# Blocks of 512 columns for the second stretch of a weight conversion, and two lasting buffers for the 16-bit exponentials in place of three

## Chip, cores and metric

One NeuronCore of one Trainium2 chip. The metric is the device time of one execution in microseconds, over all engines, from the first instruction to the last. Lower is better.

## What is computed

Three operations in a row, all in float32 at the borders, with batch 2, 768 positions, 8 heads of 64:

```python
mask = q_bucket[:, :, :, None] == k_bucket[:, :, None, :]
scores = np.where(mask, scale * q @ k.T, -1e9)
x = softmax(scores) @ v                      # (2, 768, 512) after joining heads
u = x + real(fft(fft(x, axis=1), axis=2))
un = (u - mean(u)) / sqrt(var(u) + 1e-6)
u = u + relu(un @ w_ch1) @ w_ch2             # 512 -> 2048 -> 512
out = (sigmoid(conv(u, conv_w)) * (u @ w_val)) @ w_out
```

The buckets are the signs of six projections of q and of k. The matrix products run on pairs of 16-bit numbers (a high part and the rest, three products for one), so that the result keeps the accuracy of float32. The weights arrive as 64-bit floats, read as pairs of 32-bit words.

## The kernel before

The program is written once per batch half b = 0, 1. For each half the attention runs over four head pairs g, each with three blocks i of 256 positions and two heads hh. `pair` (L312) does one head of one block: scores on TensorE (L320), their maximum on VectorE (L330), the exponential on ScalarE (L333) into `e`, then a 16-bit copy on ScalarE (L112, `a<-e`) and the rest `e - a` on GpSimd (L120, `a<-e,a`) in two halves, for each of two rows j. The finished tile `a` is transposed by a DMA from SP's queue (L346, `at<-a`). `unit_out` (L349) multiplies two transposed tiles with the values (L355, 36 matmuls), which ends a block; there are 12 blocks in each half. `prep` (L230) makes the 16-bit q and k of the next head pair in a tile `st` from the same pool as `a`, also transposed by a DMA (L247, `tb<-st`), and the bucket rows (L259, L264).

The tiles come from pools in two parts. The base part is there for both halves of the batch; `widen` adds buffers that exist for the first attention alone, and `Pool.tile` takes base and added buffers in turn. Before the change `a` has three base buffers and one added one, `at` two and two, `e` two and one.

After the attention of half 0 the mixing (`back`, L515), the norm (`norm`, L618), and the feed-forward (`ffn`, L679: first product L703, eviction L684 and L685, second product L720, eviction L691) of half 0 run beside the attention of half 1. Later come the mixing of half 1, the gating of half 0, and the feed-forward and gating of half 1.

The weights are converted in two stretches by `weights` (L414). One block is loaded into a ring by SP (L424), and for each part of a block three integer steps on VectorE (`widen`, L410 to L412) make a float32 tile `wt` from the two words. Then `split` brings it to scale and makes the two 16-bit parts:

```python
t = pool.tile([128, wp], INT32, tag="wt", name="wt", bufs=2)
k = (name, i * (r.shape[1] // wp) + c // wp)
with after_mark([marks[GATES[k]]] if k in GATES else last if PACE and not name else []):
    marks[k] = widen(t, r[:, cl, 0], r[:, cl, 1], t).ins
split(h[:, cl], l[:, cl], t.bitcast(FP32), s, how[k[1] % len(how)])
```

The first stretch takes most of `w_ch1` beside the first attention, in 12 blocks of 512 columns. The second stretch (named `w2`) takes the remaining 512 columns of `w_ch1` and all of `w_ch2` beside the mixing of half 0 and the attention of half 1, in 40 blocks of WP = 256 columns with a ring of two slots. Its `split` is "aag": two ScalarE steps (L112, `wt<-wt` and `w<-wt`) and one on GpSimd (L120, `w<-wt,w`).

What sets the order: a planner reorders each engine's instructions by dependencies and its own estimate of times. `after_mark` gives it extra edges that only bind the order; `GATES` names such edges for single blocks of the conversion (a block may not stand before a mark such as the end of the first attention, `(0, "unit", 2)`, or the first norm, `(0, "norm", 0)`). Each engine and SP's queue then work strictly in the order they are given.

## Time and profile before

| | |
|---|---|
| runs shown | 707.6, 707.6 and 710.81 us, median 707.6 |
| the profiled execution's own time | 703.61 us |
| its span | 701.8 us |
| TensorE busy | 572.9 us (82%) |
| VectorE busy | 534.5 us (76%) |
| ScalarE busy | 350.9 us (50%) |
| GpSimd busy | 313.2 us (45%) |
| mean granted TensorE clock | 0.903 |

The span is the time from the first to the last instruction in the trace; 1.8 us lie around it. Busy times are sums over the whole span, which has stages with different limits, so they say little by themselves. Windows over the span give each stage its own shares; the chain of waits follows the last instruction back to what released it.

### The profile page before, as it was taken

How to read it: one execution, taken by the hardware profiler on the slowest of the kernel's cores; microseconds unless marked ns; L12 is line 12 of the kernel's file. 1: busy time of each engine (PE TensorE's matmuls, PEld its weight loads, DVE VectorE, ACT ScalarE, POOL GpSimd, SP SyncE). 2: the span in 40 equal slices, each digit the busy share in tenths (PEclk: the TensorE clock that was granted, in tenths of full speed). 3: DMA queues.
4: the chain of work that ended last, by engine and by line, in shares of the span. 5: the costliest groups of instructions: out<-in, count | busy, mean ns of one | idle time of the engine just before them, and what ended most of it. 6: DMA issues, size and time to landing. Idle time of an engine off the chain costs nothing.

```text
span 701.8 us, 12761 instructions
## 1 busy us (share of the span) xinstructions
PE 572.9 (82%) x4958; PEld 436.3 (62%) x4958; DVE 534.5 (76%) x1002; ACT 350.9 (50%) x731; POOL 313.2 (45%) x321
## 2 busy tenths in 40 slices
PE   5775576666664769988789999799989999999997
PEld 2334353444343547666567789678767788888864
DVE  5799797997999998999875629996799346182582
ACT  4576767883866445776578725321434302121142
POOL 5665959795577722876556431455232100000000
PEclk8557878868975799999989999999999999999999
DMA  3989999999578552676875884200000000000001
GB/s 118 203 233 222 238 236 223 215 221 204 139 151 179 135 144 65 146 165 148 163 133 109 157 159 151 91 1 2 0 31 31 32 1 1 1 2 1 1 31 61
DMA packets 191804, 79.72 MB, mean 114 GB/s; under 512 B 176384, under 2 KB 182144, under 8 KB 191744
## 3 DMA queue, kind: packets, MB, share of 16 engines
q1 hardware_dynamic: 191168, 78.81, 50.6%
q8 instruction: 39, 0.64, 0.4%
q10 hardware_dynamic: 576, 0.10, 0.1%
q14 instruction: 21, 0.17, 0.1%
HBM read 32.50 MB, written 3.15 MB: 51 GB/s over the span
## 4 chain that ended last, share of the span: by engine, by line
PE 33%; DVE 27%; DMA 6%; issue 5%; POOL 4%; ACT 2%; SPq 1%; ACTq 0%; DVEq 0%; POOLq 0%
PE f L720 12%; PE f L703 10%; DMA at<-a 3%; DVE wt L412 3%; PE pv L355 2%; DVE sc L330 2%; DVE wt L411 2%; DVE wt L410 2%; DVE gt L745 2%; PE op L864 2%; POOL a L120 2%; DVE z L120 2%; DMA ring<-in_moe_w_ch_dram 2%; DVE h L685 1%; PE vp L839 1%
## 5 line engine op out<-in xcount | busy, mean ns | idle before, releaser
L120 POOL TENSOR_TENSOR a<-e,a 128x384 f16<-128x384 f32 x184 | 183.5, 1021 | 90.6 <-ACT a L112 50.6
L703 PE MATMUL f<-un,w 128*128 128x256 f16 x1152 | 134.6, 274 | 5.0 <-DVE h L685 4.7
L720 PE MATMUL f<-h,w 128*128 128x256 f16 x1152 | 132.3, 273 | 0.9 <-POOL w L120 0.9
L703 PEld LDWEIGHTS <-w 128*128 128x128 f16 x1152 | 112.7, 98 | 24.0 <-issue 7.2
L720 PEld LDWEIGHTS <-w 128*128 128x128 f16 x1152 | 111.5, 98 | 16.2 <-POOL w L120 1.4
L355 PE MATMUL pv<-at,vt 128*64 128x256 f16 x864 | 77.7, 335 | 31.3 <-DMA at<-a 21.0
L330 DVE TENSOR_SCALAR_CACHE_REDUCE sc<-sc 128x768 f32<-128x768 f32 x96 | 91.4, 961 | 14.4 <-PE sc L320 13.2
L355 PEld LDWEIGHTS <-vt 128*64 128x64 f16 x864 | 62.0, 136 | 56.4 <-issue 38.7
L333 ACT ACTIVATE e<-sc,mx 128x768 f32<-128x768 f32 x96 | 85.5, 891 | 4.1 <-POOL a L120 1.2
L320 PE MATMUL sc<-ta 96*128 96x384 f16 x192 | 54.4, 367 | 39.0 <-ACT e L333 28.6
L112 ACT ACTIVATE a<-e 128x768 f16<-128x768 f32 x96 | 79.9, 839 | 11.1 <-DMA at<-a 7.9
L685 DVE SCALAR_TENSOR_TENSOR h<-f,h 128x512 f16<-128x512 f32 x48 | 32.6, 684 | 34.4 <-ACT h L684 34.2
L320 PE MATMUL sc<-tb 128*128 128x384 f16 x192 | 56.1, 376 | 0.0
L684 ACT ACTIVATE h<-f 128x512 f16<-128x512 f32 x48 | 28.4, 591 | 49.2 <-PE f L703 49.0
L320 PEld LDWEIGHTS <-ta 96*128 96x128 f16 x192 | 17.5, 103 | 56.3 <-issue 42.0
L120 POOL TENSOR_TENSOR w<-wt,w 128x256 f16<-128x256 f32 x40 | 36.1, 910 | 32.6 <-ACT w L112 32.4
L112 ACT ACTIVATE x<-xb 128x256 f16<-128x256 f32 x24 | 11.8, 534 | 67.3 <-DVE xb L691 66.9
L331 ACT ACTIVATE mx<-mx 128x1 f32<-128x1 f32 x96 | 18.8, 197 | 52.7 <-DVE sc L330 48.1
L412 DVE SCALAR_TENSOR_TENSOR wt<-ring,wt 128x256 int32<-128x256 int32 (+1 forms) x60 | 43.3, 728 | 0.4
L691 DVE SCALAR_TENSOR_TENSOR xb<-f,xb 128x256 f32<-128x256 f32 x24 | 13.7, 615 | 37.6 <-PE f L720 37.6
L411 DVE SCALAR_TENSOR_TENSOR wt<-ring,wt 128x256 int32<-128x256 int32 (+1 forms) x60 | 41.3, 696 | 0.5
L812 DVE SCALAR_TENSOR_TENSOR gt<-xb,cw,gt 128x256 f32<-128x256 f32 x60 | 37.1, 673 | 0.0
(144 smaller groups left out, 905.5 us busy)
## 6 DMA issues: line engine op xcount, KB each, us to landing
ring<-in_moe_w_ch_dram SPq DMA_DIRECT2D x40, 256.0 KB, 3.0
ring<-in_moe_w_ch_dram SPq DMA_DIRECT2D x12, 512.0 KB, 4.4
lv<-in_v_dram SPq DMA_DIRECT2D x8, 384.0 KB, 3.7
out_dram<-ob SPq DMA_DIRECT2D x12, 256.0 KB, 2.0
lq<-in_q_dram SPq DMA_DIRECT2D x7, 384.0 KB, 3.8
lk<-in_k_dram SPq DMA_DIRECT2D x7, 384.0 KB, 4.2
ring<-in_moe_w_val_dram SPq DMA_DIRECT2D x4, 512.0 KB, 4.2
ring<-in_moe_w_out_dram SPq DMA_DIRECT2D x4, 512.0 KB, 3.5
```

What stands on the lines that cost most here:

```text
L112: return nc.scalar.activation(out=o, in_=i, func=ACTF.Copy, scale=s)
L120: return (nc.gpsimd if eng == "g" else nc.vector).tensor_tensor(out=o, in0=i0, in1=i1, op=op)
L320: nc.tensor.matmul(out=s[:, n, 0:384], lhsT=z[0:rows, 0, hh, r], rhs=z[0:rows, 1, hh, n * 384:n * 384 + 384], start=(x == 0), stop=(x == 1),)
L330: last[:] = [nc.vector.tensor_scalar(s, s, -(PEN * PEN) / 2, None, ALU.max, ALU.max, accum_out=m[:, 0:1]).ins]
L333: marks["first", 2 + j] = nc.scalar.activation(out=e.rearrange("p (a b) -> p a b", a=2), in_=s, func=ACTF.Exp, bias=m[:, 1:2], scale=SC, a ...
L355: nc.tensor.matmul(out=p[64 * hh:64 * hh + 64, :], lhsT=va[g][:, hh, c, x, :], rhs=at[hh][:, :, y, c, :], start=(c == 0 and n == 0), stop= ...
L411: nc.vector.scalar_tensor_tensor(out=tmp, in0=hi, scalar=-0x40000000, in1=tmp, op0=ALU.bitwise_and, op1=ALU.bitwise_or)
L412: return nc.vector.scalar_tensor_tensor(out=dst, in0=lo, scalar=29, in1=tmp, op0=ALU.logical_shift_right, op1=ALU.bitwise_or)
L685: nc.vector.scalar_tensor_tensor(out=h[:, 1, f:f + 2, :], in0=p, scalar=0.0, in1=h[:, 0, f:f + 2, :], op0=ALU.max, op1=ALU.subtract)
L703: nc.tensor.matmul(out=p[:, o, :], lhsT=w1[:, i, kd, (f + o) * 128:(f + o) * 128 + 128], rhs=un[:, j, kd, :], start=(k == 0), stop=(k == 3 ...
L720: nc.tensor.matmul(out=p[:, o, :], lhsT=w2[:, i, f, (d + o) * 128:(d + o) * 128 + 128], rhs=h[:, j, f, :], start=(k == 0), stop=(k == 3 * ...
L812: nc.vector.scalar_tensor_tensor(out=o, in0=src, scalar=cw[:, d, j:j + 1].bitcast(FP32), in1=o, op0=ALU.mult, op1=ALU.add)
```

## The change

The second stretch takes its blocks 512 columns wide, in a ring of two slots of twice the size, with `wt` tiles of 512 columns. The `a` pool gives one of its three base buffers to the added part: it has two and two, still four for the first attention, and two for the second. The gates are rewritten for the new block numbers.

```diff
-GATES = {('w2', 18): (0, 'norm', 0), ('w2', 6): (0, 'unit', 2), ('w2', 36): (0, 'unit', 0), ('w2', 22): (0, 'unit', 1), ('w2', 20): (0, 'unit', 2)}
+GATES = {("w2", 3): (0, "unit", 2), ("w2", 9): (0, "norm", 0)}
...
-        pools = AttnPools(base, ld=2, ta=2, tb=1, vt=2, e=2, a=3, at=2, sm=4, sc=2, pv=1, bt=1)
+        pools = AttnPools(base, ld=2, ta=2, tb=1, vt=2, e=2, a=2, at=2, sm=4, sc=2, pv=1, bt=1)
...
-        pools.widen(att, ld=1, tb=1, e=1, a=1, at=2, sc=1)
+        pools.widen(att, ld=1, tb=1, e=1, a=2, at=2, sc=1)
...
-            list(w_blocks(w_ch1, w1, W1S, WP, DFF - LEFT)) + list(w_blocks(w_ch2, w2, W2S, WP)), slots(wst.tile([128, 2, 2 * WP], INT32, name="ring2")), wst, HOW[1], name="w2"
+            list(w_blocks(w_ch1, w1, W1S, WB, DFF - LEFT)) + list(w_blocks(w_ch2, w2, W2S, WB)), slots(wst.tile([128, 2, 2 * WB], INT32, name="ring2")), wst, HOW[1], WB, "w2"
```

The planner then orders the whole program anew. Three places show it.

VectorE, just ahead of the first norm's last step (L670), before the change (`stat` is the norm's variance, `xb_67` takes the mixing's sums, `wt<-ring` are the conversion's steps):

```order
L657 TENSOR_TENSOR stat<-stat 128x2
L411 SCALAR_TENSOR_TENSOR wt<-ring_1920,wt 128x256
L600 TENSOR_TENSOR xb_67<-mp,xb_67 128x2x128
L658 TENSOR_TENSOR stat<-stat 128x2
L412 SCALAR_TENSOR_TENSOR wt<-ring_1920,wt 128x256
L659 TENSOR_SCALAR stat<-stat 128x2
L600 TENSOR_TENSOR xb_67<-mp,xb_67 128x2x128
L660 TENSOR_TENSOR stat<-stat 128x2
L410 TENSOR_SCALAR wt<-ring_1920 128x256
L411 SCALAR_TENSOR_TENSOR wt<-ring_1920,wt 128x256
L412 SCALAR_TENSOR_TENSOR wt<-ring_1920,wt 128x256
L670 TENSOR_TENSOR cen<-cen,rstd 128x512 x2
```

The same place with the change:

```order
L654 TENSOR_SCALAR stat<-var 128x2
L600 TENSOR_TENSOR xb_67<-mp,xb_67 128x2x128
L657 TENSOR_TENSOR stat<-stat 128x2
L658 TENSOR_TENSOR stat<-stat 128x2
L600 TENSOR_TENSOR xb_67<-mp,xb_67 128x2x128
L659 TENSOR_SCALAR stat<-stat 128x2
L660 TENSOR_TENSOR stat<-stat 128x2
L600 TENSOR_TENSOR xb_67<-mp,xb_67 128x2x128
L670 TENSOR_TENSOR cen<-cen,rstd 128x512 x2
```

The conversion's steps have left the norm; 17 whole blocks of 256 stood ahead of L670, now 9 of 512 do, all of them earlier.

SP's queue beside the later blocks of the second attention, before the change (`ring_1920` are the loads of the second stretch):

```order
L247 DMA_TRANSPOSE tb<-st 128x24x128
L424 DMA ring_1920<-in_moe_w_ch_dram 128x512 x8
L346 DMA_TRANSPOSE at<-a 128x24x128
L424 DMA ring_1920<-in_moe_w_ch_dram 128x512 x2
L346 DMA_TRANSPOSE at<-a 128x24x128
L424 DMA ring_1920<-in_moe_w_ch_dram 128x512 x4
L346 DMA_TRANSPOSE at<-a 128x24x128 x2
L424 DMA ring_1920<-in_moe_w_ch_dram 128x512 x3
L346 DMA_TRANSPOSE at<-a 128x24x128
L213 DMA lv<-in_v_dram 128x2x384
L424 DMA ring_1920<-in_moe_w_ch_dram 128x512
L247 DMA_TRANSPOSE tb<-st 128x24x128
```

With the change:

```order
L247 DMA_TRANSPOSE tb<-st 128x24x128
L424 DMA ring_1920<-in_moe_w_ch_dram 128x1024 x6
L346 DMA_TRANSPOSE at<-a 128x24x128
L424 DMA ring_1920<-in_moe_w_ch_dram 128x1024 x2
L346 DMA_TRANSPOSE at<-a 128x24x128
L424 DMA ring_1920<-in_moe_w_ch_dram 128x1024
L346 DMA_TRANSPOSE at<-a 128x24x128 x4
L213 DMA lv<-in_v_dram 128x2x384
L247 DMA_TRANSPOSE tb<-st 128x24x128
L346 DMA_TRANSPOSE at<-a 128x24x128 x12
```

Behind the last of these loads now stand 17 transpositions (16 of `a`, one of `st`) and one load of values, where 12 transpositions stood behind it before.

SP's queue at the start of the program (one piece of the difference):

```order
 L213 DMA lq<-in_q_dram 128x2x384
 L213 DMA lv<-in_v_dram 128x2x384
+L247 DMA_TRANSPOSE tb<-st 128x24x128
 L346 DMA_TRANSPOSE at<-a 128x24x128
-L247 DMA_TRANSPOSE tb<-st 128x24x128
 L213 DMA lk<-in_k_dram 128x2x384
 L938 DMA cf<-in_dft_f_dram 128x1536
```

The first tile of `st` is now transposed ahead of the first tile of `a`.

On TensorE, the order counts these feed-forward matmuls (L703 and L720) ahead of the end of each block of the second attention: at the 16th block's end 176 before and 215 now, at the 19th 354 and 406, at the 23rd 576 and 625, at the 24th 654 and 703.

## Rows read from the trace of the kernel before

**Rows 1.** Chain of waits: start us, us, what; first and a later feed-forward run.
```profile
260.93 5.04 PE f L703 x38
...
581.51 20.96 PE f L703 x192
```

**Rows 2.** TensorE's timeline (start us, us, instruction): value products of blocks 16, 19, 24.
```profile
300.00 2.15 PE L355 MATMUL pv<-at,vt 128*64 128x256 f16 x35
...
356.77 4.00 PE L355 MATMUL pv<-at,vt 128*64 128x256 f16 x35 [0.95 <-DMA at<-a]
...
418.35 2.12 PE L355 MATMUL pv<-at,vt 128*64 128x256 f16 x35 [0.43 <-DMA at<-a]
```

**Rows 3.** Windows: stretch, length, busy PE, PEld, DVE, ACT, POOL, clock, DMA, GB/s.
```profile
176.00:260.90 84.90, 51.21 (x445) 35.73 (x443) 82.49 (x164) 50.89 (x108) 55.06 (x53) 0.77 0.64 147
260.90:302.20 41.30, 39.70 (x317) 30.17 (x315) 37.21 (x77) 26.46 (x62) 21.36 (x26) 0.98 0.44 114
302.20:361.00 58.80, 43.59 (x415) 32.28 (x413) 51.68 (x92) 37.85 (x89) 37.37 (x40) 0.95 0.75 151
361.00:421.00 60.00, 58.85 (x592) 47.51 (x590) 28.43 (x56) 38.97 (x86) 29.22 (x33) 1.00 0.77 146
421.00:475.00 54.00, 47.66 (x468) 41.97 (x467) 51.43 (x103) 21.27 (x30) 19.36 (x19) 1.00 0.24 79
475.00:702.00 227.00, 217.42 (x1875) 179.43 (x1872) 136.59 (x273) 60.05 (x113) 27.34 (x20) 1.00 0.04 15
```

**Rows 4.** SP's timeline: the transpositions of the last two blocks.
```profile
396.76 7.47 SPq L346 DMA_TRANSPOSE at<-a  x2
...
408.43 8.05 SPq L346 DMA_TRANSPOSE at<-a  x2
```

**Rows 5.** Windows of tile wt alone: stretch, length, busy DVE, ACT, POOL, clock, DMA.
```profile
176.00:260.90 84.90, 29.86 (x51) 13.55 (x34) 19.79 (x17) 0.77 0.64 147
260.90:302.20 41.30, 13.14 (x32) 7.37 (x20) 6.55 (x10) 0.98 0.44 114
302.20:361.00 58.80, 22.62 (x38) 10.49 (x26) 9.08 (x12) 0.95 0.75 151
```

**Rows 6.** Lines L410 to L412, 176 to 262 and 421 to 480: ns min/median/max.
```profile
L410 DVE TENSOR_SCALAR wt<-ring x17: 275/547/1709, 176.3 to 257.0; 128x256 int32<-128x256 int32 x17
...
L411 DVE SCALAR_TENSOR_TENSOR wt<-ring,wt x17: 406/421/1140, 178.3 to 257.3; 128x256 int32<-128x256 int32 x17
...
L412 DVE SCALAR_TENSOR_TENSOR wt<-ring,wt x17: 390/419/1137, 179.0 to 257.8; 128x256 int32<-128x256 int32 x17
...
L410 DVE TENSOR_SCALAR wt<-ring x8: 408/420/833, 427.1 to 455.5; 128x512 int32<-128x512 int32 x8
...
L411 DVE SCALAR_TENSOR_TENSOR wt<-ring,wt x8: 674/686/694, 429.0 to 457.2; 128x512 int32<-128x512 int32 x8
...
L412 DVE SCALAR_TENSOR_TENSOR wt<-ring,wt x8: 670/680/1034, 432.0 to 459.2; 128x512 int32<-128x512 int32 x8
```

**Rows 7.** Groups by line and form, 0 to 176: busy us, mean ns.
```profile
L412 DVE SCALAR_TENSOR_TENSOR wt<-ring,wt 128x512 int32<-128x512 int32 x12 | 12.9, 1073 | 0.1
...
L411 DVE SCALAR_TENSOR_TENSOR wt<-ring,wt 128x512 int32<-128x512 int32 x12 | 12.0, 1000 | 0.1
L410 DVE TENSOR_SCALAR wt<-ring 128x512 int32<-128x512 int32 x12 | 7.9, 654 | 0.1
```

**Rows 8.** ScalarE's timeline: first copy into the last tile a.
```profile
405.06 0.84 ACT L112 ACTIVATE a<-e 128x768 f16<-128x768 f32 x1
```

**Rows 9.** Chain of waits: the last tile's second subtractions and its transposition.
```profile
409.07 2.25 POOL a L120 x2
...
412.81 5.50 DMA at<-a
```

**Rows 10.** Who waited for whom, 176 to 262: us in total, times, longest.
```profile
ACT a L112 <- DMA at<-a: 4.5, 2, 3.6
```

**Rows 11.** SP's timeline: the first transposition of a.
```profile
23.21 3.75 SPq L346 DMA_TRANSPOSE at<-a  x1
```

## Prediction

> **What bounds the kernel now.** I read the page first, then the chain of waits, then cut the span from 176 us (the end of the first attention) into six spans by events of the chain: 260.9, the first feed-forward matmul [rows 1]; 302.2 and 361, the ends of the 16th and the 19th block of value products (two pairs of a head pair each); 421, the end of the 24th and last [rows 2]; 475, where the second mixing has its sums. The windows give each span's limit [rows 3].
>
> - A, 176 to 260.9 (first mixing and first norm): VectorE is busy 82.49 of 84.90 us. It is the limit, and what it is freed of comes off the span.
> - B, 260.9 to 302.2: TensorE 39.70 of 41.30, VectorE 37.21. Two limits side by side.
> - C, 302.2 to 361: VectorE 51.68 of 58.80, TensorE only 43.59. TensorE is short of work that VectorE is late with.
> - D, 361 to 421: TensorE 58.85 of 60, VectorE 28.43. The order on TensorE is full, and a loop has the same length: the two transpositions of a block start at 396.76, those of the next at 408.43 [rows 4], 11.7 us later. Two lasting `at` buffers mean that the next block's first transposition waits for the value products, which wait for the second transposition to land.
> - E, 421 to 475: VectorE 51.43 of 54. F, 475 to the end: TensorE 217.42 of 227.
>
> **The change, part by part.** *Conversion.* The 40 blocks of 256 columns become 20 of 512, with the same bytes and the same six steps. Up to the first norm the two VectorE orders hold the same instructions, except that 17 whole blocks of 256 become 9 of 512. The 17 took 29.86 us in A, 1.76 each [rows 5]. Undisturbed a block of 256 takes 0.275 + 0.406 + 0.390 = 1.07 us and one of 512 0.408 + 0.674 + 0.670 = 1.75 [rows 6], so 0.69 of each 1.76 was contention. What nine cost: if contention goes by instruction, 9 x (1.75 + 0.69) = 21.9; at the mean of 512-column blocks in the first stretch (0.654 + 1.000 + 1.073 = 2.73) [rows 7], 24.5; if it goes by column, 15.8 + 17 x 0.69 x 18/17 = 28.2. I take 24.5, a measurement of this very shape. **A: -5.4 us** (-8.0 to -1.7). ScalarE (13.55 us of A) and GpSimd (19.79) [rows 5] also take half as many steps, but both idle a third of A [rows 3] under VectorE's work, so I cost that at nothing; in B GpSimd's longer steps come back as the upper price there.
>
> Why contention might grow: a VectorE step with two inputs has a median of 0.421 us and a maximum of 1.140 [rows 6], so a step mostly runs free or waits some 0.7 us, about one GpSimd instruction. The Trainium skill, SBUF — State Buffer, section "Who interferes with whom", says that a VectorE instruction with two SBUF inputs and a GpSimd instruction that reads SBUF exclude each other for the whole of the one that came first. By that rule the wait lengthens with the blocks, A gains the 1.7 of the bound, and the edit gains least where it was meant to gain; the two-valued durations agree with it, while the first stretch's 2.73 lies between the two prices.
>
> *Order in B.* The new order puts more into B: 215 feed-forward matmuls before the 16th block's end where there were 176. At 20.96/192 = 0.109 us each [rows 1] that is 39 x 0.109 = 4.3 us of TensorE, so 45.6 if TensorE sets it. On VectorE it holds 32 conversion steps as before, but of 512 columns: 13.14 us [rows 5] become 18.7 undisturbed (32 x 1.75/3) to 29.1 (32 x 2.73/3), and one score reduction leaves (some 1.1), so VectorE needs 41.7 to 52.1. I take 48 for B. **+6.7** (+4.3 to +10.8).
>
> *C without conversion.* Of the 38 steps (22.62 us) [rows 5] one is left. VectorE falls to 30, TensorE's work grows by 13 matmuls (191 for 178) to 45.0. The loop of transpositions needs 3 x 11.7 = 35. I take TensorE's 45 and 3 for waits on the two preparations that lie here: 48 for 58.8. **-10.8** (-13.8 to 0: should the waits of C not be VectorE's).
>
> *The buffer.* For the second attention `a` has two lasting buffers instead of three; the first keeps four in all. What is known: the last tile is first written at 405.06 [rows 8], its subtractions end at 411.3 and its transposition lands at 418.3 [rows 9], a lifetime of 13.2 us. Two tiles per block in two buffers would give one block per 13.2 us, where the loop asks for 11.7. But part of this lifetime is slack: between the two copies of a tile the engine did other things. From the rows: a buffer comes free when a transposition lands, 5.5 us after its start [rows 9]; the next tile then needs two copies and the subtractions, a copy of 0.84 [rows 8] and two pairs of subtractions of 2.25 [rows 9], 5.3 us, so it is ready 10.8 us after that start, 0.9 before the loop wants it. Nothing is lost if ScalarE is on time. It is busy 38.97 of 60 in D [rows 3], and it works in order: behind a copy that waits stand the exponentials and the evictions of the feed-forward, and TensorE waits for those. With three buffers ScalarE was once held up by a transposition for 3.6 us [rows 10]. So the price per block is 0 to 3.6 us; I take 1 for the five blocks of D, where the loop is tight, because the single steps, with their 0.9 of slack, are nearer to what happens there than one wait of another span. D keeps its own work (297 matmuls for 300). **+5** (0 to +18).
>
> *Tail.* At the end of attention the feed-forward stands 49 matmuls further (703 for 654), 5.3 us that TensorE need not do later. Of these 25 lay in E, which VectorE bounds, and 24 in F (2.6 us). **-4** (-5.3 to -2.6).
>
> *Loads.* 20 loads of twice the size replace 40 on SP's queue; fewer issue slots stand between transpositions, and I cost this at nothing: in A, where the conversions are densest, VectorE idles 2.4 us in all [rows 3], so the loads come under its work. If that cover went, VectorE would show waits for the ring.
>
> *Start.* The planner swapped the first transposition of `a` and that of `st` on SP; one is 3.75 us [rows 11]. One result comes that much earlier, one later, so the bound is -3.7 to +3.7, and I take 0: neither the work nor the four buffers of the first attention have changed.
>
> Sum: -5.4 + 6.7 - 10.8 + 5 - 4 = -8.5 us. Against the profiled execution's own 703.61 us that is 695.1. Its own time lies 4.0 under the median of the runs, 707.6, and I give the forecast on the median's footing: **699 us**.
>
> **The rivals.**
>
> 1. *Slower: two `a` buffers set the pace.* Place: ScalarE's first copy into a tile, C and D, eight blocks. Every us per block costs 8; with 5 already in the sum, the gain is gone at (8.5 + 5)/8 = 1.7 us and the time is over 711 at 2.1. At the one wait seen, 3.6 us in every block, it is 8 x 3.6 = 28.8 in place of 5: +15.3, 723 us. For it: the lifetime of 13.2 against a period of 11.7, and TensorE in D with no room. Against: the tile ready 0.9 us ahead by the single steps, and an order that was planned for two buffers.
> 2. *Faster by more: nothing of it binds.* A -5.4, B 45.6 (+4.3), C 45 (-13.8), no price for the buffer, tail -5.3: -20.2, 687 us. For it: VectorE's busy shares in A and C. Against: C has two preparations whose transpositions and moves TensorE waits for.
> 3. *No change: contention by column.* A VectorE step that meets a GpSimd instruction waits for its end, the instruction is twice as long now, and so A's gain falls to 1.7 and B fills to VectorE's 52.1 (+10.8): -1.7 + 10.8 - 10.8 + 5 - 4 = -0.7, 707 us. The Trainium skill's section named above states this kind of exclusion. For it: 2.73 a block in the first stretch against 1.75 undisturbed. Against: half the instructions can only meet half as many GpSimd instructions if those do not grow as well.
> 4. *The edit does not do what it says:* C was not VectorE's, and what leaves VectorE there turns into idle time. Without C's term the sum is +2.3, 710 us, still no change.
>
> **How the numbers follow.** About 0.5% (3.5 us) is what a measurement of this kernel can tell from no change, so faster means below 704.1 and slower above 711.1. The forecast has 0.50 and rival 2 0.14: faster 0.64. Rivals 3 and 4 share 0.17: same. Rival 1 has 0.19: slower. The range goes from 686, just under rival 2, to 712, over the no-change cases and the smallest prices of rival 1; what it leaves out is most of rival 1 and a little below, under 0.2. The likeliest case's own range, A to tail with the mid bounds, is 692 to 704.
>
> **What would show it right or wrong.** In the profile after: the first feed-forward matmul near 255.5 (A); 20 blocks with a VectorE mean sum between 2.0 and 2.7 us (3 if 2.7 or more); the 19th block's end some 9 us earlier than 361 and VectorE well under 40 us busy between the 16th and the 19th; late blocks 11.7 to 13 us apart. Wrong it would be if ScalarE's copies into `a` show waits for transpositions of over 2 us per block, or if the end of attention does not come before 418 while the tail stays 281 us long.

## Result, and the profile after

The changed kernel takes 711.93 us (median of 7 runs, 708.9 to 713.55) where the kernel before takes 707.6 (median of 7, 706.71 to 710.81). The ratio is 1.0059 with a 95% interval of 1.0038 to 1.008: slower by some 4 us, where 8.5 us less was forecast. The profiled execution after has an own time of 708.9 us and a span of 707.1, 5.3 more than before on both counts.

The page after, busy times over the whole span:

```profile
PE 574.0 (81%) x4958; PEld 438.4 (62%) x4958; DVE 531.9 (75%) x942; ACT 346.4 (49%) x691; POOL 305.1 (43%) x301
```

VectorE's, ScalarE's and GpSimd's fell a little and TensorE's hardly moved, so the added time is in waits. The windows after, cut at the same events as in [rows 3] (first feed-forward matmul, ends of the blocks 16, 19 and 24):

```profile
176.00:264.90 88.90, 48.70 (x401) 34.98 (x398) 80.63 (x134) 45.01 (x83) 49.34 (x43) 0.69 0.62 144
...
264.90:313.40 48.50, 45.24 (x354) 34.29 (x351) 47.52 (x77) 31.25 (x63) 27.44 (x25) 0.96 0.53 142
313.40:364.10 50.70, 44.89 (x429) 33.67 (x428) 34.34 (x60) 30.39 (x64) 29.14 (x30) 0.93 0.64 118
364.10:424.70 60.60, 57.81 (x587) 46.94 (x584) 27.28 (x55) 38.66 (x85) 28.07 (x32) 1.00 0.72 131
```

B came out near the forecast, C is 2.8 us longer than it, and D grew by 0.9 us where 5 had been priced. A went the other way: it ends at 264.9 instead of 260.9, and VectorE, which idled 2.4 us of A before, now idles 88.90 - 80.63 = 8.3. Its conversion did get cheaper there (tile wt alone; busy DVE, ACT, POOL), 23.00 us where [rows 5] have 29.86:

```profile
176.00:264.90 88.90, 23.00 (x29) 11.20 (x18) 14.52 (x9) 0.69 0.62 144
...
264.90:313.40 48.50, 22.02 (x29) 11.48 (x19) 10.27 (x8) 0.96 0.53 142
313.40:364.10 50.70, 1.79 (x3) 1.85 (x3) 3.42 (x3) 0.93 0.64 118
```

So VectorE was freed of 6.9 us and the stretch became longer. TensorE's timeline after, the value products that end the blocks 16, 19 and 24, answers to [rows 2]:

```profile
311.28 2.15 PE L355 MATMUL pv<-at,vt 128*64 128x256 f16 x35
...
361.98 2.12 PE L355 MATMUL pv<-at,vt 128*64 128x256 f16 x35 [0.40 <-DMA at<-a]
...
422.55 2.15 PE L355 MATMUL pv<-at,vt 128*64 128x256 f16 x35
```

More of one kind of wait shows on ScalarE, and a slower pace on SP. ScalarE's timeline after, copies into a new tile `a` that waited for an earlier tile's transposition (in brackets the wait in us; five of nine, 13.3 us in all); before, there were two such waits in the second attention, 4.5 us in all [rows 10]:

```profile
185.67 1.58 ACT L112 ACTIVATE a<-e 128x768 f16<-128x768 f32 x2 [0.65 <-DMA at<-a]
...
198.29 1.58 ACT L112 ACTIVATE a<-e 128x768 f16<-128x768 f32 x2 [4.61 <-DMA at<-a]
...
209.95 1.58 ACT L112 ACTIVATE a<-e 128x768 f16<-128x768 f32 x2 [0.86 <-DMA at<-a]
...
346.07 1.58 ACT L112 ACTIVATE a<-e 128x768 f16<-128x768 f32 x2 [1.92 <-DMA at<-a]
...
382.08 0.84 ACT L112 ACTIVATE a<-e 128x768 f16<-128x768 f32 x1 [2.13 <-DMA at<-a]
```

SP's timeline, the first four transpositions of `a` in the second attention, before:

```profile
185.09 3.67 SPq L346 DMA_TRANSPOSE at<-a  x1
192.90 4.33 SPq L346 DMA_TRANSPOSE at<-a  x1
204.87 4.32 SPq L346 DMA_TRANSPOSE at<-a  x1
210.69 4.16 SPq L346 DMA_TRANSPOSE at<-a  x1
```

and after:

```profile
179.93 3.57 SPq L346 DMA_TRANSPOSE at<-a  x1
191.98 4.67 SPq L346 DMA_TRANSPOSE at<-a  x1
204.48 3.58 SPq L346 DMA_TRANSPOSE at<-a  x1
216.21 3.64 SPq L346 DMA_TRANSPOSE at<-a  x1
```

Before they come (210.69 - 185.09)/3 = 8.5 us apart; after, 12.1. They start 5 us earlier, since the first attention ends earlier (its 12th block at 174.8 instead of 178.2), and the fourth is 5.5 later. The question for the experiments: is this the lost buffer, the wide blocks, their new place, or only a new order?

### The profile page after: what moved, and what is told of

Same layout as the page of the kernel before. It is cut to its first block, busy times and chain, and to the rows that moved or that the text cites. A ratio compares the mean times of both kernels' runs of the same rounds, so it can differ in the third digit from the quotient of the medians.

```text
span 707.1 us, 12553 instructions
## 1 busy us (share of the span) xinstructions
PE 574.0 (81%) x4958; PEld 438.4 (62%) x4958; DVE 531.9 (75%) x942; ACT 346.4 (49%) x691; POOL 305.1 (43%) x301
## 5 line engine op out<-in xcount | busy, mean ns | idle before, releaser
L120 POOL TENSOR_TENSOR a<-e,a 128x384 f16<-128x384 f32 x184 | 186.6, 1039 | 100.4 <-ACT a L112 84.1
L703 PE MATMUL f<-un,w 128*128 128x256 f16 x1152 | 135.6, 274 | 2.4 <-DVE h L685 1.0
L720 PE MATMUL f<-h,w 128*128 128x256 f16 x1152 | 134.1, 275 | 0.5 <-DVE h L685 0.5
L703 PEld LDWEIGHTS <-w 128*128 128x128 f16 x1152 | 112.9, 98 | 20.8 <-issue 4.0
L720 PEld LDWEIGHTS <-w 128*128 128x128 f16 x1152 | 113.1, 99 | 17.4 <-issue 2.3
L355 PE MATMUL pv<-at,vt 128*64 128x256 f16 x864 | 73.7, 322 | 35.5 <-DMA at<-a 20.5
L112 ACT ACTIVATE a<-e 128x768 f16<-128x768 f32 x96 | 79.2, 837 | 22.3 <-DMA at<-a 15.1
L355 PEld LDWEIGHTS <-vt 128*64 128x64 f16 x864 | 59.7, 131 | 46.5 <-issue 31.5
L112 ACT ACTIVATE x<-xb 128x256 f16<-128x256 f32 x24 | 11.7, 534 | 56.1 <-DVE xb L691 55.3
L412 DVE SCALAR_TENSOR_TENSOR wt<-ring,wt 128x512 int32<-128x512 int32 x40 | 38.8, 975 | 0.3
L120 POOL TENSOR_TENSOR w<-wt,w 128x512 f16<-128x512 f32 x20 | 28.2, 1418 | 22.4 <-ACT w L112 22.3
L411 DVE SCALAR_TENSOR_TENSOR wt<-ring,wt 128x512 int32<-128x512 int32 x40 | 37.2, 938 | 0.3
```

The costliest lines, as they stand in the source:

```text
L112: return nc.scalar.activation(out=o, in_=i, func=ACTF.Copy, scale=s)
L120: return (nc.gpsimd if eng == "g" else nc.vector).tensor_tensor(out=o, in0=i0, in1=i1, op=op)
L355: nc.tensor.matmul(out=p[64 * hh:64 * hh + 64, :], lhsT=va[g][:, hh, c, x, :], rhs=at[hh][:, :, y, c, :], start=(c == 0 and n == 0), stop= ...
L411: nc.vector.scalar_tensor_tensor(out=tmp, in0=hi, scalar=-0x40000000, in1=tmp, op0=ALU.bitwise_and, op1=ALU.bitwise_or)
L412: return nc.vector.scalar_tensor_tensor(out=dst, in0=lo, scalar=29, in1=tmp, op0=ALU.logical_shift_right, op1=ALU.bitwise_or)
L703: nc.tensor.matmul(out=p[:, o, :], lhsT=w1[:, i, kd, (f + o) * 128:(f + o) * 128 + 128], rhs=un[:, j, kd, :], start=(k == 0), stop=(k == 3 ...
```

## The experiments

All ratios are to runs of the kernel before that were taken beside the kernel's own. The planner orders the whole program anew with every edit, so single edits are not pure; from the second set on the same edit was made in several orders. "A" is `a` lasting + added buffers, "steps" the columns of one conversion step, "f" the feed-forward matmuls ahead of the end of the second attention, "end" that end in the profiled execution, "tail" its own time less that end, "wait" ScalarE's waits for transpositions of `a` between 176 and 430 us (copies into `a` and `st`).

| kernel | A | steps | ratio, 95% interval | f | end | tail | wait |
|---|---|---|---|---|---|---|---|
| before | 3+1 | 256 | 1 | 654 | 420.5 | 283.1 | 4.5 |
| after | 2+2 | 512 | 1.0059, 1.0038 to 1.008 | 703 | 424.7 | 284.2 | 13.3 |
| buf2 | 2+2 | 256 | 1.0081, 1.0057 to 1.0105 | 654 | 428.4 | 284.2 | 15.7 |
| parts256 | 2+2 | 256 | 1.0021, 1.0005 to 1.0038 | 654 | 423.2 | 283.5 | 7.4 |
| mixgate5 | 2+2 | 512 | 1.008, 1.0061 to 1.01 | 703 | 427.0 | 285.7 | 14.5 |
| gate6 | 2+2 | 512 | 1.0146, 1.0121 to 1.017 | 727 | 428.3 | 288.0 | 19.3 |
| turn1 | 3+1 | 256 | 1.0084, 1.0055 to 1.0114 | 693 | 429.1 | 281.5 | 2.4 |
| turn2 | 3+1 | 256 | 1.011, 1.0088 to 1.0132 | 693 | 431.7 | 280.0 | none |
| turn3 | 3+1 | 256 | 0.9952, 0.9933 to 0.9971 | 654 | 420.7 | 283.3 | 0.5 |
| aturn1 | 2+2 | 512 | 1.0111, 1.0086 to 1.0135 | 710 | 432.3 | 284.8 | 14.8 |
| s1 | 2+2 | 512 | 1.015, 1.0129 to 1.0171 | 803 | 436.6 | 281.1 | 15.1 |
| s2 | 2+2 | 512 | 1.0024, 1.0011 to 1.0036 | 657 | 425.5 | 283.3 | 10.5 |
| bs2 | 3+1 | 256 | 0.9977, 0.9962 to 0.9991 | 654 | 421.5 | 283.6 | 4.1 |
| bs3 | 3+1 | 256 | 1.0088, 1.0056 to 1.0121 | 576 | 425.0 | 287.8 | 4.5 |
| buf2s2 | 2+2 | 256 | 1.0071, 1.0051 to 1.0092 | 576 | 425.7 | 287.3 | 15.0 |
| parts256s2 | 2+2 | 256 | 1.0082, 1.006 to 1.0103 | 572 | 425.7 | 288.9 | 7.5 |
| t3s2 | 3+1 | 256 | 1.0014, 0.9998 to 1.003 | 630 | 421.4 | 286.7 | 0.7 |
| buf2t3 | 2+2 | 256 | 1.0127, 1.0106 to 1.0149 | 630 | 427.8 | 286.8 | 16.2 |
| one512 | 3+1 | 512 | 1.0151, 1.012 to 1.0181 | 467 | 415.8 | 300.2 | none |

### One part at a time

**buf2**, on the kernel before:

```diff
-        pools = AttnPools(base, ld=2, ta=2, tb=1, vt=2, e=2, a=3, at=2, sm=4, sc=2, pv=1, bt=1)
+        pools = AttnPools(base, ld=2, ta=2, tb=1, vt=2, e=2, a=2, at=2, sm=4, sc=2, pv=1, bt=1)
...
-        pools.widen(att, ld=1, tb=1, e=1, a=1, at=2, sc=1)
+        pools.widen(att, ld=1, tb=1, e=1, a=2, at=2, sc=1)
```

> The kernel before with one edit: the a pool has two lasting buffers and two added ones instead of three and one; blocks stay 256 columns wide, gates as before. Theory 1 (the lost lasting buffer costs the time; wide blocks would have gained): slower than before by 5 us or more, about 713 to 718 us, ScalarE's copies into a waiting for transpositions 10 us or more longer in all than in the kernel before (7.9 us), and the longest waits between the first mixing and the first feed-forward matmul. Theory 2 (the nine wide blocks that now stand ahead of the mixing's first sum delay the norm; the buffer costs nothing): within 2 us of before, about 708. Theory 3 (each replanned order moves the time by some us either way, whatever was edited): anything within 5 us, with no wait that grows as theory 1 says.

1.0081: as much as the whole change or more, and ScalarE's waits are 15.7 us where they were 4.5. Theory 1, in this order (its 712.5 us lie just under the 713 expected). But the first feed-forward matmul comes at 262.6, only 1.7 us later than before, while the attention ends 7.9 later: the buffer's price does not all show in A. A confound was noticed here: the first attention was faster with the new order (its last block ends at 176.3 instead of 178.2), as in the change.

**mixgate5**, on the changed kernel:

```diff
-GATES = {("w2", 3): (0, "unit", 2), ("w2", 9): (0, "norm", 0)}
+GATES = {("w2", 3): (0, "unit", 2), ("w2", 5): (0, "mix", 0, 0), ("w2", 9): (0, "norm", 0)}
```

> The changed kernel with one more gate: block 5 of the second stretch may not stand ahead of the first sum of the mixing. On VectorE 5 blocks of 512 instead of 9 then stand ahead of that sum, still 9 ahead of the last step of the first norm; the buffers are as in the change, and TensorE's feed-forward counts ahead of the ends of the blocks of the second attention are the same 215, 406 and 703. Theory 2: the first sum comes some 4 x 2.5 = 10 us earlier (242.5 to about 232), the first feed-forward matmul 5 to 9 us earlier (264.9 to about 256 to 260), and the time falls by as much, to about 703 to 707 us. Theory 1: the first mixing is held by transpositions that come late, so the norm hardly moves: first feed-forward matmul within 2 us of 264.9, time about 711.

The first sum did come 7.4 us earlier (235.1), but the norm's mean came later (256.5 for 254.4) and the first feed-forward matmul at 268.8, 3.9 later than in the change. The place of the wide blocks ahead of the first sum is not what holds A: theory 2 falls. Theory 1's matmul within 2 us of 264.9 did not come either.

**parts256**, on the changed kernel:

```diff
-GATES = {("w2", 3): (0, "unit", 2), ("w2", 9): (0, "norm", 0)}
+GATES = {("w2", 6): (0, "unit", 2), ("w2", 18): (0, "norm", 0)}
...
-            list(w_blocks(w_ch1, w1, W1S, WB, DFF - LEFT)) + list(w_blocks(w_ch2, w2, W2S, WB)), slots(wst.tile([128, 2, 2 * WB], INT32, name="ring2")), wst, HOW[1], WB, "w2"
+            list(w_blocks(w_ch1, w1, W1S, WB, DFF - LEFT)) + list(w_blocks(w_ch2, w2, W2S, WB)), slots(wst.tile([128, 2, 2 * WB], INT32, name="ring2")), wst, HOW[1], WP, "w2"
```

> The changed kernel's loads of 512 columns and its buffers, but the conversion steps work on halves of 256 columns (two wt tiles per load), with the gates on the same places (parts 6 and 18). The planner puts 11 parts of 256 ahead of the first mixing sum (9 before the change, 18 worth with it) and 18 ahead of the norm's last step. Theory 1 (buffer): about as slow as the changed kernel or slower, 711 to 718, since the buffer is gone and the instruction overhead is not saved. Theory 2 (place of the wide blocks): about as before, 706 to 709, first feed-forward matmul near 261. The 256-column steps on VectorE should again cost 1.76 us per part beside the first mixing, against 2.5 for 512.

1.0021: faster than the change, where theory 1 had it no faster. Its 707.8 us are theory 2's number, but the first feed-forward matmul comes at 265.4 and not near 261, so theory 2's reason is not there. It has the fewest waits of the two-buffer kernels (7.4 us). Against buf2 it shows that an edit as slight as the size of the loads and the gates, with its new order, shifts the time by 0.6%.

**gate6**, on the changed kernel:

```diff
-GATES = {("w2", 3): (0, "unit", 2), ("w2", 9): (0, "norm", 0)}
+GATES = {("w2", 3): (0, "unit", 2), ("w2", 6): (0, "norm", 0)}
```

> The changed kernel with the norm's gate at block 6 instead of 9: six blocks of 512 stand ahead of the first mixing sum and of the norm's last step, and the other fourteen behind it. Theory 2: the first feed-forward matmul comes 3 x 2.5 = 7.5 us earlier, near 257, the next stretch (to the end of the 16th block) has three more blocks for VectorE, which limits it, and so gives 5 to 7.5 back; time 707 to 712. Theory 1: no gain at the norm, the same three blocks later: 711 to 716.

The first matmul comes at 258.4, as theory 2 had it, but the time is 1.0146, beyond both theories: 727 feed-forward matmuls stand ahead of the attention's end, and the tail is longest of the first set.

### How much an order is worth

**turn1**, **turn2** and **turn3** are the kernel before with one line, 1, 2 or 3, after the call that adds buffers; **aturn1** is the changed kernel with 1:

```diff
+        pools.a.turn = 1
```

> The kernel before (256-column blocks, three lasting a buffers and one added) with one line: the first attention takes its a buffers from the second on (the added one comes third instead of fourth). Nothing is added or taken away, but the planner orders anew, and the first transposition of st now goes ahead of that of a, as in the change. The kernels with two lasting buffers so far end the first attention 3.4 to 5.8 us earlier than the kernel before, and then lose 8.5 to 11.7 us to the end of the second attention. If the gain at the start is the order's and the loss is the buffer's: first attention over near 166 (170.6 before), second attention 250 us long as before, time 702 to 704, faster than before. If both are only what any new order brings (theory 3): first attention near 170 or the second 255 or longer, time 705 to 713.

> The kernel before with one line: the first attention takes its a buffers from the third on. The start again has the transposition of st ahead of that of a, and the rest of the order is like that of the kernel with the second buffer first. Buffer theory: first attention near 166, second 250 us, time 702 to 704. Theory 3: 705 to 713. Any wait of ScalarE's copies into a for transpositions should stay near the 7.9 us of before, since three buffers last.

> The kernel before with one line: the first attention takes the added a buffer first. The planner orders anew, but the first transposition of a stays ahead of that of st, as in the kernel before. It is the control: the same buffers, the same blocks, another order. If the order of the start is what gives 4 us, this one does not have them: first attention near 170 or 171, time 706 to 709. Theory 3: up to 5 us off either way.

> The changed kernel (512-column blocks, two lasting a buffers) with the same one line: the first attention starts with the second of the four a buffers. The planner orders anew. If two lasting buffers cost 8 to 11 us in the second attention whatever the order: from the end of the first attention to that of the second 258 to 262 us as in the other two-buffer kernels, ScalarE's copies waiting 13 us or more for transpositions, time 708 to 717. Theory 3: the second attention may also come out at 250 to 255 us.

Here theory 3 is right, and its size was put too low: with the same work, blocks and buffers, three orders gave 1.0084, 1.011 and 0.9952, the first two (714.0 and 715.1 us) above its 713. Both orders that start like the change were slower, and the first attention did not end earlier in them (its last block at 182.1 and 181.0); so the swap at the start does not by itself bring the gain that nearly all two-buffer kernels show there. So a single comparison of two edits says nothing under about 1% here. What did not depend on the order is the wait: 0 to 4.5 us in all kernels with three lasting buffers, 7.4 to 19.3 in all with two.

### Work ahead of the attention's end, and matched pairs

**s1** and **s2** are the changed kernel, **bs2** and **bs3** the kernel before, with one constant (s1; s2 and bs2; bs3):

```diff
-START, F0FIRST, WFIRST = ("norm", 0), 0, 1
+START, F0FIRST, WFIRST = ("norm", 1), 0, 1
...
+START, F0FIRST, WFIRST = ("mix", 2, 3), 0, 1
...
+START, F0FIRST, WFIRST = ("mix", 0, 0), 0, 1
```

> The changed kernel with one constant: the program starts to write the units of the second attention after the second norm mark instead of the first, so the planner puts 803 feed-forward matmuls ahead of the end of that attention instead of 703. Blocks, buffers and gates as in the change. Theory O (what stands ahead of the attention's end delays it, and the tail from there on is set by the second mixing and norm on VectorE, so that nothing comes back): attention ends 100 x 0.109 = 10.9 us later, near 435, tail unchanged at 280 to 283 in its own time, time about 720 to 723. Theory N (moves of feed-forward work are neutral, as the tail term of the prediction has it): the tail gets 8 to 11 us shorter, time 710 to 714.

> The changed kernel with the same constant set the other way: the second attention's units are written from the last sum of the first mixing on. 657 feed-forward matmuls then stand ahead of the attention's end (703 in the change, 654 before), 63 instead of 215 ahead of the end of its 16th block. Nine blocks of 512 ahead of the first mixing sum, two lasting buffers: as in the change. Theory O: attention ends some 5 us earlier than in the change (near 419 to 420), tail unchanged, time 705 to 708. Buffer theory: the two buffers bind the denser attention all the more, time 711 or more. Theory N: 710 to 714.

> The kernel before (256-column blocks, three lasting buffers) with the constant as in the kernel that writes the second attention from the last mixing sum on: 654 feed-forward matmuls ahead of the attention's end, as in the kernel before, but 48 instead of 176 ahead of its 16th block. Theory O (only the count ahead of the end matters): within 2 us of before, 706 to 710. It also is the partner of the same edit on the changed kernel: the difference of the two is what blocks of 512 with two buffers are worth at the same count of feed-forward work; the prediction without its tail and order terms would have the changed one 5 to 10 us faster, the buffer theory has it 5 or more slower.

> The kernel before with the constant set to the first sum of the first mixing: 576 feed-forward matmuls ahead of the end of the second attention instead of 654. Theory O: the attention ends 78 x 0.109 = 8.5 us earlier, near 412, and the work that is put off finds room beside the second mixing, where VectorE sets the pace: time 699 to 703. Theory N, or a tail in which TensorE has no room: the tail grows by the same 8.5 us, time 706 to 710.

In s1 the attention ends at 436.6, 11.9 us later than in the change for 10.9 of feed-forward work, and the tail gives back 3.1 of them; its 717.1 us lie between the two theories. In bs3, with 8.5 us of work put off, the tail grows by 4.7 and the attention ends later all the same; its 713.5 us fit neither theory's number. So of work moved across the attention's end the tail took up 28% (s1) and 55% (bs3). The change put 49 matmuls ahead of that end and its tail is 1.1 us longer.

s2 against bs2, the same constant and almost the same count (657 and 654), is the whole change without its extra feed-forward work: 1.0024 against 0.9977, 0.5% slower again, 3.3 us where the buffer theory had 5 or more.

The last set made the buffer edit and the step edit in these orders: **buf2s2** and **parts256s2** are buf2 and parts256 with START as in bs2, **t3s2** is turn3 with that START, **buf2t3** is buf2 with the turn of turn3.

> The kernel before with the second attention written from the last sum of the first mixing on, and with two lasting a buffers instead of three (256-column blocks). Its partner with three buffers took 0.9977 of the kernel before; 576 feed-forward matmuls stand ahead of the attention's end (654 there). Buffer theory: ScalarE's copies and preparations wait 8 us or more for transpositions between 176 and 430 us (4.1 in the partner), and the time is 3 to 8 us over the partner: 708 to 713. Theory 3 (only the order matters): such waits grow but the time is within 3 us of 705.

> The kernel with two lasting a buffers alone (256-column blocks), with the first attention taking an added buffer ahead of the others in the same place as the fastest order of three buffers does. 630 feed-forward matmuls ahead of the attention's end. Its partner with three buffers took 704.0. Buffer theory: 3 to 8 us over it, 707 to 712, with waits of ScalarE's copies for transpositions of 8 us or more between 176 and 430 (0.5 in the partner). Theory 3: anywhere between 702 and 716.

> The changed kernel's loads of 512 columns and two lasting buffers, conversion steps on halves of 256, and the second attention written from the last sum of the first mixing on. 572 feed-forward matmuls ahead of the attention's end. Against the same with steps of 512 columns (1.0024 of before) it tells what 512-column steps are worth with two buffers. If the steps save what the prediction says, this one is slower by 4 us or more, 712 to 716; if their saving on VectorE is lost to waits, within 2 us of 708.5; if the wide steps hurt, 704 to 707.

> The kernel before (three lasting buffers, 256-column blocks) with two constants: the first attention takes the added a buffer first (0.9952 of before by itself), and the second attention is written from the last sum of the first mixing on (0.9977 by itself). If the two gains add, 702 us; ScalarE's waits for transpositions stay under 5 us between 176 and 430. Theory 3: between 702 and 712, without any wait that tells.

The buffer costs time in each pair: 1.0081 against 1; 1.0071 against 0.9977; 1.0127 against 0.9952. That is 0.8, 0.9 and 1.8%, or 6, 7 and 12 us, and the intervals of no pair touch. The totals alone do not prove it, for the orders of a pair differ too: only buf2 and before have the same count f. bs3, with three buffers and the 576 matmuls of buf2s2, takes as long as buf2s2 (1.0088 and 1.0071). t3s2 and buf2t3 have the same 630, though another START, and differ by 1.1%; buf2t3's 716.7 us lie above both theories' ranges.

The stretch from the end of the 12th block to that of the 16th does not hang on what stands behind it. The kernels below (all with steps of 256 columns but s2) have nearly equal counts of feed-forward matmuls ahead of the 16th block's end within each set, 15 and 23 apart at most, which is 1.6 and 2.5 us:

| START | lasting buffers | stretch, us (feed-forward matmuls) |
|---|---|---|
| as in bs2 | 3 | bs2 109.1 (48), t3s2 110.8 (57) |
| as in bs2 | 2 | buf2s2 118.4 (54), parts256s2 119.4 (55), s2 120.5 (63) |
| as before | 3 | before 123.9 (176), turn3 124.8 (182), turn1 125.2 (181), turn2 129.2 (181) |
| as before | 2 | buf2 130.0 (168), buf2t3 135.0 (174), parts256 135.7 (191) |

With two buffers this stretch is 8 to 11 us longer in the first set, with either width of the steps, and 1 to 12 in the second, where new orders of three buffers already lie 5 apart. This is the surest sign of the buffer's price, and it lies ahead of C and D. A part of it is won back by the first attention's earlier end: in the three pairs the 16th block ends 4.2, 6.8 and 2.7 us later.

Who waited for whom between 176 and 430 us (total, times, longest), bs2:

```profile
ACT a L112 <- DMA at<-a: 4.1, 2, 3.2
```

buf2s2:

```profile
ACT a L112 <- DMA at<-a: 12.6, 8, 3.9
ACT st L112 <- DMA at<-a: 2.4, 2, 1.4
```

turn3:

```profile
ACT a L112 <- DMA at<-a: 0.5, 1, 0.5
```

buf2t3:

```profile
ACT a L112 <- DMA at<-a: 13.8, 9, 2.4
ACT st L112 <- DMA at<-a: 2.4, 1, 2.4
```

The wide steps, with two buffers, gain little: after against buf2 is 1.0059 against 1.0081 (intervals overlap), s2 against buf2s2 1.0024 against 1.0071, s2 against parts256s2 1.0024 against 1.0082. The first pair gives 1.6 us, the others 3 to 4, but s2 has 657 matmuls ahead of the attention's end and the other two 576 and 572; with after against parts256 the sign turns (1.0059 against 1.0021). Two gains of orders do not add (t3s2, 1.0014).

### Wide steps with three buffers

Three lasting buffers and the full ring of wide blocks do not fit the memory together. **one512** makes room otherwise, on the changed kernel:

```diff
-                t = pool.tile([128, wp], INT32, tag="wt", name="wt", bufs=2)
+                t = pool.tile([128, wp], INT32, tag="wt", name="wt", bufs=1 if name else 2)
...
-        pools = AttnPools(base, ld=2, ta=2, tb=1, vt=2, e=2, a=2, at=2, sm=4, sc=2, pv=1, bt=1)
+        pools = AttnPools(base, ld=2, ta=2, tb=1, vt=2, e=2, a=3, at=2, sm=4, sc=2, pv=1, bt=1)
...
-        pools.widen(att, ld=1, tb=1, e=1, a=2, at=2, sc=1)
+        pools.widen(att, ld=1, tb=1, e=1, a=1, at=2, sc=1)
...
-slots(wst.tile([128, 2, 2 * WB], INT32, name="ring2"))
+slots(wst.tile([128, 1, 2 * WB], INT32, name="ring2"))
```

> The changed kernel's 512-column steps with three lasting a buffers: room for the third is made by a ring of one slot and one wt tile for the second stretch, so that each block waits for its load and the conversion runs late (only 264 feed-forward matmuls ahead of the 19th block's end, 467 ahead of the last). Its time is therefore no measure, 715 to 740. What is looked at is the stretch from the end of the first attention to the first feed-forward matmul: if the two buffers set the pace there, the first four transpositions of the second attention come 8 to 9.5 us apart as with three buffers and 256-column steps (11 to 12.5 with two buffers in every order), and ScalarE waits under 5 us for transpositions between 176 and 430. If the wide steps set it, they come 11 us or more apart here too.

Its conversion runs late and its tail is 300.2 us, as expected. SP's timeline, the first four transpositions of its second attention:

```profile
184.74 9.54 SPq L346 DMA_TRANSPOSE at<-a  x2
200.35 3.68 SPq L346 DMA_TRANSPOSE at<-a  x1
206.36 3.96 SPq L346 DMA_TRANSPOSE at<-a  x1
```

(206.36 - 184.74)/3 = 7.2 us apart (8 to 9.5 were expected, and 11 or more if the wide steps set the pace), and ScalarE waits for none between 176 and 430. The first feed-forward matmul comes at 255.0, and VectorE is again busy for nearly all of that stretch:

```profile
173.00:262.00 89.00, 58.62 (x513) 40.91 (x511) 83.42 (x148) 49.75 (x91) 47.79 (x43) 0.77 0.63 145
```

(It has fewer blocks ahead of the norm than the change, 6 for 9, so 255.0 is not what the change would have had with a third buffer. gate6, which also has 6, but two buffers, has its first feed-forward matmul at 258.4.) With buf2, which has narrow steps and two buffers, SP's timeline gives the other corner:

```profile
181.41 3.59 SPq L346 DMA_TRANSPOSE at<-a  x1
192.07 3.64 SPq L346 DMA_TRANSPOSE at<-a  x1
204.33 4.22 SPq L346 DMA_TRANSPOSE at<-a  x1
218.66 4.11 SPq L346 DMA_TRANSPOSE at<-a  x1
```

12.4 us apart. Worked out alike, the other two-buffer kernels have 11.1 (aturn1) to 12.5 (buf2s2), with either size of step; the other three-buffer kernels have 8.3 (t3s2) to 8.9 (turn2). The spacing belongs to the buffer and not to the width of the steps.

**A version that beats both** is turn3: 703.98 us median, 0.9952 of the kernel before (0.9933 to 0.9971). It is another order of the same work, not a use of the wide blocks.

## Why the prediction was wrong

In the profiled execution, term by term, forecast and measured against before (each to the ends of the same blocks):

| term | forecast | measured |
|---|---|---|
| start | 0 (-3.7 to +3.7) | first attention's last block 3.4 earlier |
| A, to the first feed-forward matmul | -5.4 (-8.0 to -1.7) | +4.0 |
| B | +6.7 (+4.3 to +10.8) | +7.3 |
| C | -10.8 (-13.8 to 0) | -8.0 |
| buffer, in D | +5 (0 to +18) | +0.9 |
| tail | -4 (-5.3 to -2.6) | +1.1 |
| sum | -8.5 | +5.3 |

**The step that failed is the buffer's price: how many buffers are left for `a`, and where that is felt; with it fails A.** The prediction wrote "C and D, eight blocks" and left A to VectorE: "It is the limit, and what it is freed of comes off the span". It costed A's conversion well: nine blocks of 512 were put at 24.5 us, and the wt window shows 23.00. But the first three blocks of the second attention lie in A as well, and "Two tiles per block in two buffers" took both buffers to be free for `a`. They are not, for `st` comes from the same pool. In the changed kernel one `st` is written ahead of the second attention's first tile, and its transposition is issued behind that of the fourth (ScalarE's and SP's timelines):

```profile
163.19 0.84 ACT L112 ACTIVATE st<-lq 128x768 f16<-128x768 f32 x1 [2.35 <-DMA at<-a]
...
219.91 3.75 SPq L247 DMA_TRANSPOSE tb<-st  x1
```

It lands at 225.4. Until then one buffer is left for `a`, and a tile can only start when the one before it has landed. That is what the copies shown above do: those at 185.67, 198.29 and 209.95 start 0.02 us after the landing of the transpositions issued at 179.93, 191.98 and 204.48. So the 12.1 us between tiles are the lifetime of one tile (11.6 to 12.8 us for the first four). The prediction's lifetime, 13.2 us, was about right; it was shared out over two tiles in flight where there was one. In mixgate5 a copy into `a` is seen to wait for `st` itself:

```profile
226.67 0.84 ACT L112 ACTIVATE a<-e 128x768 f16<-128x768 f32 x1 [0.66 <-DMA tb<-st]
```

With three lasting buffers two were left. In the kernel before, the fourth and the fifth tile started when the second and the third had landed (issued at 192.90 and 204.87), not one tile later:

```profile
199.10 0.84 ACT L112 ACTIVATE a<-e 128x768 f16<-128x768 f32 x1 [0.95 <-DMA at<-a]
...
211.18 0.84 ACT L112 ACTIVATE a<-e 128x768 f16<-128x768 f32 x1 [3.58 <-DMA at<-a]
```

There a tile lived 13 to 18 us, and two in flight gave one per 8.5. All 19 kernels agree: with two lasting buffers the second to the fifth tile each start 0.02 to 0.7 us after the landing of the tile before; with three they start 3 to 12 us ahead of it, but never ahead of the landing of the tile before that one. The sign that was there to read is [rows 10]: ScalarE's two waits with three buffers lay in A, and each was for the last tile but one, so only two of the three buffers served `a`. The longer one was used as the upper price for D.

What this did to A shows at its end. TensorE's value products waited 9.7 us for transpositions in A (2.2 before), and work was put off. The last 19.9 us of A, before and after:

```profile
241.00:260.90 19.90, 13.09 (x154) 9.53 (x153) 18.89 (x39) 8.14 (x18) 8.52 (x10) 0.95 0.47 116
```

```profile
245.00:264.90 19.90, 18.34 (x195) 14.68 (x194) 14.83 (x31) 5.69 (x8) 3.83 (x4) 0.82 0.30 74
```

Before, VectorE was the limit here; after, it is TensorE, with 195 matmuls for 154 and a granted clock of 0.82 for 0.95. Who VectorE waited for in A after:

```profile
DVE xb L600 <- PE mp L592: 4.6, 6, 1.3
DVE sc L330 <- PE sc L320: 2.9, 1, 2.9
DVE wt L410 <- POOL w L120: 2.8, 1, 2.8
```

So what VectorE was freed of turned into idle time. How much of A's miss is the buffer's alone is not settled. From the first attention's last block to the first feed-forward matmul VectorE idles 2.1 us before, 6.7 in buf2 and 9.5 in the change (among all kernels with START as before, 2.1 to 5.9 with three buffers and 6.7 to 12.7 with two). Of the 4.0 us by which A ends later, buf2 has 1.7; the other 2.3 came with the wide steps or with their order.

**The buffer's size was about right, its place wrong.** 5 us were forecast, and buf2 alone costs 6 by its ratio, 7 and 12 in two other orders. That the size is near is luck: it was worked out for D. In D the waits are what was priced, 5.3 us over five waits (1.06 per block), but D is only 0.9 longer. Rival 1, two `a` buffers that set the pace, is nearest to the mechanism; it put the place in C and D, missed `st`, and had it at 0.19. It is luck, too, that 711.9 us lie just inside the range, whose upper end, 712, was set by rival 1's smallest prices in C and D.

**B and C** came as worked out: the conversion left C, VectorE's busy time fell from 51.68 to 34.34 us, and C took 50.7 us where 48 was forecast. Rival 4 (C is not VectorE's) is out.

**The signs.** Of those that the prediction named, the conversion's was right (2.0 to 2.7 us a block forecast, 23.00 us for nine blocks and two first steps measured) and so was C's VectorE under 40; the last two blocks end 11.5 us apart, where 11.7 to 13 was named; the first feed-forward matmul was to come at 255.5 and came at 264.9, and the last sign of a miss is there: the attention ends at 424.7, not before 418, with the tail as long as it was. The other, ScalarE's copies waiting over 2 us per block, did not show (13.3 us for twelve blocks): a copy that is held in A may cost more than its own wait, since the mixing's copies and the exponentials stand behind it, but no run separates that.

**The tail was the second wrong term.** The prediction took 24 matmuls off TensorE's busy tail. The chain of waits after runs through VectorE in the second norm, whose steps (cen, stat) stand among those of the gating (gt):

```profile
522.20 6.47 DVE gt L745 x12
...
535.97 1.08 DVE cen L635
537.05 0.33 DVE gt L752
537.38 3.07 DVE x L126 x4
...
542.43 4.35 DVE gt L745 x11
546.79 0.07 DVE stat L654
```

The windows from the attention's end on, before and after:

```profile
420.50:702.00 281.50, 265.58 (x2348) 221.71 (x2343) 188.51 (x375) 81.38 (x142) 46.70 (x38) 1.00 0.08 27
```

```profile
424.70:707.00 282.30, 262.96 (x2299) 218.83 (x2294) 195.37 (x373) 80.86 (x142) 43.94 (x38) 0.99 0.09 30
```

TensorE is busy 2.6 us less and idles 3.4 us more: the saved work turned into waiting. s1 shows it with twice the dose: 100 matmuls (10.9 us) less to do, 3.1 us gained.

**The start** was put at 0 as "neither the work nor the four buffers of the first attention have changed". The first attention ended 3.4 us earlier. That the swap of two transpositions alone does not do it is borne out by turn1 and turn2, which have the swap and no gain; what in the new order does it stays open.

**Contention** (rival 3) can be settled from rows. In A after, groups by line and form (busy us, mean ns):

```profile
L412 DVE SCALAR_TENSOR_TENSOR wt<-ring,wt 128x512 int32<-128x512 int32 x9 | 9.5, 1060 | 0.0
L411 DVE SCALAR_TENSOR_TENSOR wt<-ring,wt 128x512 int32<-128x512 int32 x9 | 8.6, 952 | 0.1
L410 DVE TENSOR_SCALAR wt<-ring 128x512 int32<-128x512 int32 x11 | 5.1, 470 | 2.8 <-POOL w L120 2.8
```

A block is 1.060 + 0.952 + 0.470 = 2.48 us, 0.73 over the undisturbed 1.75 of [rows 6]; a block of half the size had 0.69 over. Contention went by instruction and not by column, so rival 3's price for A (28.2 us, 23.00 measured) is out, though the 707 us that it gave were nearer to the result than the 699 of the forecast. The Trainium skill, SBUF — State Buffer, section "Who interferes with whom", says that a VectorE step with two SBUF inputs and a GpSimd instruction that reads SBUF shut each other out for the whole of the one that came first. The loss per step, 0.24 us on the mean, did not grow with the width here, so what the prediction drew from that rule is not borne out. That does not go against the rule: of GpSimd's 43 instructions in A after, only nine are the conversion's wide ones. Whether the exclusion is whole, these rows do not tell.

**What stays open:** what the full change would take with a third lasting buffer was not tried, since both do not fit the memory; nor was a version in which `st` gives its buffer back earlier, or has one of its own, which is what the reading above points to; and the size of the wide steps' own gain, -3 to +4 us in the pairs, lies within what a new order moves.

## What to carry to other kernels

When a buffer is given up, list every tile that takes buffers from its pool and how long each holds one: a tile that waits long for its turn leaves the others fewer buffers than the pool has. The lifetime of a tile over the tiles that are really in flight gives the pace, and a wait for a buffer in the old profile, read with whose landing ended it, tells how many those are. An engine that is 97% busy may still stand just ahead of the next limit, so before its savings are taken off the span, check what else paces that stretch. Where a planner reorders the program with each edit, make the edit in two or three orders before believing a difference of under 1%.

## What the runs showed that was not expected

- The same work with the same buffers, only differently ordered, ranged from 0.9952 to 1.011 of the kernel before (turn3 and turn2), nearly three times the size of the change's effect.
- A pool's buffers did not all serve the tile that it is named for: in the changed kernel `st` held one of the two lasting `a` buffers from 163.2 to 225.4, from ahead of the second attention's first tile to behind its fourth.
- Work moved off a TensorE that was busy 217 of 227 us came back in the tail by 28% (s1) and 55% (bs3) only.
- In A the mean granted clock (1 is the upper of its two levels, 2.4 GHz, 0.5 the lower, 1.2) fell from 0.77 to 0.69 while TensorE's busy time went from 51.21 of 84.90 us to 48.70 of 88.90. buf2 kept 0.77, with 46.77 of 86.30 from its first attention's last block to its first feed-forward matmul. What the clock adds to A was not separated.
